# Reading the moving operand of the float32r products from its two halves in turn, in an attention and MLP kernel

## The chip, the cores and the metric

One core of a Trainium2 chip runs the whole kernel. The metric is the device time in microseconds (us) of one execution; the rearranging of inputs and outputs by numpy, ahead of the launch and behind it, is not in it. A time is the median of several executions. For this kernel a difference under 0.3% can't be told from no change.

## The reference

```python
# B, S, D = 4, 3008, 256; z has 64 features; D_FF = 2048
scores = (1.0 / S) * np.matmul(z, z.transpose(0, 2, 1))   # per batch, 3008 x 3008
attn = np.maximum(scores, 0.0) ** 2
x = (u * np.matmul(attn, v)).reshape(B * S, D)
h = x @ w_in
g = h * np.clip(h + 3.0, 0.0, 6.0) / 6.0
y = g @ w_out
```

All of it is float32. The output y has 12032 rows of 256.

## The kernel before

Everything is computed transposed: tokens lie along the free dimension, features along the 128 partitions. TensorE's products are in float32r. To keep float32's precision each operand is split into a rounded high part and the rest (`ah`/`al`, `vh`/`vl`, `xh`/`xl`, `gh`/`gl`, `wi` and `wo` with both parts in one tile), and each product is the sum of three matmuls: low by high, high by low, high by high. All matmuls are made by the helper `mm` (line 75), so in the profile every matmul has line 75 and is known by its tiles.

The tokens of a batch are cut into six chunks of columns: five of 512 and one of 448. For a chunk, the keys are walked in 12 pairs of 128-row blocks. Per pair there are

- the scores (`scores`, `first_scores`): two matmuls `s<-zy,zx` and `s<-zx` for each of the two blocks, into a PSUM bank; then Relu on ScalarE (line 433) from PSUM into the SBUF tile `rt`; then squares on ScalarE and VectorE and the split into `ah`, `al`. The score matrix is symmetric, so many pairs are not computed: the squares of an earlier chunk are kept in DRAM (`keep`), fetched back and transposed on VectorE (`turn`, `from_mirror`). A few pairs are mirrored in one half and computed in the other: the half pairs, whose scores are matmuls of 256 columns (`from_mirror`).
- the product with v (`av`, `first_av`): 12 matmuls `o<-ah,vl`, `o<-ah,vh`, `o<-al,vh` of 512 or 448 columns, that sum over all pairs in the banks `o0`, `o1`. At the end of a chunk, `times_u` multiplies with u (tile `u`).

The MLP runs on pairs of chunks. With the two chunks' columns as halves of 512 or 480 columns, and two halves of the features, `group` does a 2 by 2 block product in seven products instead of eight (`product`, 21 matmuls `m<-xh,wi` and `m<-xl,wi` in all, each with 512 or 480 columns), ScalarE and VectorE put the sums and the gate together in `ra`, `rb`, split them into `gh`, `gl`, and `downs_of` multiplies with `w_out` (matmuls `y<-gh,wo`, `y<-gl,wo`).

The order of the instructions on each engine is written out by hand at the end of the function: the scores run two pairs ahead of the product with v, and from pair 33 on (`MLP_FROM`) one MLP unit is spread over every three pairs; what is left of the MLP runs at the end. Up to that point VectorE also turns the weights, that come as float64, into float32 pieces. Each matmul has its own weight load (PEld in the profile), so there are 8426 of each; ten of these are a warm-up at the start.

The moving operand (`rhs`) of every matmul is read in its natural order: 512 (480, 448, 256) neighbouring float32 words of each partition, one after the other.

Of the kernel before, what the change touches and what calls it, by code (L numbers as in the profile page):

```python
# [10 lines left out]
AF = mybir.ActivationFunctionType  # L11
ALU = mybir.AluOpType

B, S, D, DQK, DFF = 4, 3008, 256, 64, 2048
NT = B * S
P = 128
CH = 512
NCH = 6
# [4 lines left out]
NFP = NF // 2  # L23
# [18 lines left out]
def relu2_attention_then_hswish_mlp(  # L42
# [9 lines left out]
    nc = tc.nc  # L52
# [20 lines left out]

    def mm(out, lhsT, rhs, start, stop, part=False):
        nc.tensor.matmul(out, lhsT=lhsT, rhs=rhs, start=start, stop=stop, skip_group_check=part)  # L75

    def sub(out, a, b):
        nc.vector.tensor_tensor(out=out, in0=a, in1=b, op=ALU.subtract)  # L78
# [337 lines left out]
    def scores(b, c, p, square_on="da", banks="xx"):  # L416


        if is_mirrored(b, c, p):
            yield from from_mirror(b, c, p, banks[1])  # L420
            return
        n = width(c)
        zx, zy = (z[:, :n] for z in zt[b, c])
        rt = rpool.tile([P, 2, CH], F32, tag="r", name="rt")
        rn = rt[:, :, :n]
        for r in range(2):
            s = ps.tile([P, CH], F32, tag=banks[r], name="s")
            j = 2 * p + r
            cols = slice((j % 4) * P, (j % 4) * P + P)
            zj = zt[b, j // 4][0][:, cols]  # L430
            mm(s[:, :n], zj, zy, True, False)
            mm(s[:, :n], zj, zx, False, True)
            nc.scalar.activation(out=rn[:, r], in_=s[:, :n], func=AF.Relu, scale=1.0 / S)  # L433
            if not r:
                yield
        ah = apool.tile([P, 2, CH], F32R, tag="ah", name="ah")
        al = apool.tile([P, 2, CH], F32R, tag="al", name="al")
        hn, ln = ah[:, :, :n], al[:, :, :n]
        keeps = p // 2 > c and (b, p // 2, c) not in DIRECT or is_half(b, c, p + 1) and p // 2 == c
        r2, r_of, r2_of, h_of, l_of = rn, rn, rn, f(hn), ln  # L440
        if keeps or square_on != "aa":
            r2 = r2_of = rpool.tile([P, 2, CH], F32, tag="r", name="r2")[:, :, :n]
        if keeps:
            r_of, r2_of = in_order(rn), by_quadrant(r2)
            h_of, l_of = in_order(f(hn)), in_order(ln)

        def square(on, rows):
            to, of = (r2_of[:, rows], r_of[:, rows])
            if on == "a":
                nc.scalar.activation(out=to, in_=of, func=AF.Square)  # L450
            else:
                nc.vector.tensor_tensor(out=to, in0=of, in1=of, op=ALU.mult)  # L452

        half = 4 if keeps else 1
        if square_on[0] == square_on[1] == "d":
            square("d", slice(None))
        elif square_on[0] == "d":
            square("d", slice(0, half))
        nc.scalar.activation(out=hn, in_=rn, func=AF.Square)  # L459
        if square_on[0] == "a":  # L460
            square("a", slice(None))
        elif square_on[1] == "a":
            square("a", slice(half, None))
        flush_copies()
        if keeps:
            keep(b, c, p, r2)
        yield
        if p < NPAIR - 1:
            sub(l_of, r2_of, h_of)
        else:  # L470
            first, second = (slice(0, 4), slice(4, 8)) if keeps else (0, 1)
            to = in_order(hn) if keeps else hn
            sub(l_of[:, first], r2_of[:, first], h_of[:, first])
            sub(to[64:128, second], r2_of[64:128, second], h_of[64:128, second])
        at[b, c, p] = (ah, al)
        yield

    def first_scores():

        zx, zy = zt[0, 0]  # L480
        rt = rpool.tile([P, 2, CH], F32, tag="r", name="rt")
        r2 = rpool.tile([P, 2, CH], F32, tag="r", name="r2")
        ah = apool.tile([P, 2, CH], F32R, tag="ah", name="ah")
        al = apool.tile([P, 2, CH], F32R, tag="al", name="al")
        at[0, 0, 0] = (ah, al)
        for r in range(2):
            s = ps.tile([P, CH], F32, tag="xy"[r], name="s")
            zj = zx[:, r * P:(r + 1) * P]
            mm(s, zj, zy, True, False)
            mm(s, zj, zx, False, True)  # L490
            nc.scalar.activation(out=rt[:, r], in_=s, func=AF.Relu, scale=1.0 / S)
            nc.scalar.activation(out=ah[:, r], in_=rt[:, r], func=AF.Square)
            nc.vector.tensor_tensor(out=r2[:, r], in0=rt[:, r], in1=rt[:, r], op=ALU.mult)
            sub(al[:, r], r2[:, r], f(ah[:, r]))

    def first_av():

        for d in range(2):
            ot[d] = ps.tile([P, CH], F32, tag=f"o{d}", name=f"o{d}")
        ah, al = at[0, 0, 0]  # L500
        vh, vl = vt[0, 0]
        for k, (a, w, r) in enumerate(
            [(ah, w, r) for r in range(2) for w in (vl, vh)] + [(al, vh, r) for r in range(2)]
        ):
            for d in range(2):
                mm(ot[d], w[:, r, d * P:(d + 1) * P], a[:, r], k == 0, False)

    def width(c):
        return CH if c < NCH - 1 else S - CH * (NCH - 1)
# [1 line left out]
    ot = {}  # L511

    def av(b, c, p, d):

        n = width(c)
        first = p == pairs_of(b, c)[0]
        if first:
            home = f"y0{d}" if (b, c) == (0, 1) else f"o{d}"
            ot[d] = ps.tile([P, CH], F32, tag=home, name=f"o{d}")
        o = ot[d][:, :n]  # L520
        ah, al = at[b, c, p]
        vh, vl = vt[b, p]
        dd = slice(d * P, d * P + P)
        last = p == NPAIR - 1
        passes = [(w, ah, r) for r in range(2) for w in (vl, vh)]
        passes += [(vh, al, r) for r in range(1 if last else 2)]
        for k, (w, a, r) in enumerate(passes):
            mm(o, w[:, r, dd], a[:, r, :n], first and k == 0, last and k == len(passes) - 1)

    raw_x = {}  # L530

# [18 lines left out]
    xt = {}  # L550
# [56 lines left out]
    def downs_of(i, q, gs):  # L607

        n = tokens(i)[1] // 2

        def last_one(h, e):
            o = yt_t[h, e]
            gh, gl = gs[h]
            ee = slice(e * P, e * P + P)
            w = wo[i, q]
            y = rpool.tile([P, 2, CH], F32, tag="r", name="y")[:, e, :n]
            order = (1, 0) if h else (0, 1)
            for r in order:
                mm(o[:, :n], w[:, 1, r, ee], gh[:, r, :n], False, False)
                mm(o[:, :n], w[:, 0, r, ee], gh[:, r, :n], False, False)  # L620
                mm(o[:, :n], w[:, 0, r, ee], gl[:, r, :n], False, r == order[1])
            if e:
                nc.vector.tensor_scalar(
                    out=y, in0=o[:, :n], scalar1=1.0 / 6.0, scalar2=None, op0=ALU.mult
                )
            else:
                nc.scalar.activation(out=y, in_=o[:, :n], func=AF.Copy, scale=1.0 / 6.0)
            t0 = tokens(i)[0] + h * n
            nc.sync.dma_start(out=yt[e * P:(e + 1) * P, t0:t0 + n], in_=y)

        if (i, q) == (NPR - 1, NFP - 1):
            return [(h, e, last_one) for h in range(2) for e in range(2)]

        def one(h, e):
            if q == 0:
                yt_t[h, e] = ps.tile([P, CH], F32, tag=f"y{h}{e}", name=f"y{h}{e}")
            o = yt_t[h, e][:, :n]
            gh, gl = gs[h]
            ee = slice(e * P, e * P + P)
            w = wo[i, q]  # L640
            for r in range(2):
                mm(o, w[:, 1, r, ee], gh[:, r, :n], q == 0 and r == 0, False)
                mm(o, w[:, 0, r, ee], gh[:, r, :n], False, False)
            for r in range(2):
                mm(o, w[:, 0, r, ee], gl[:, r, :n], False, q == NFP - 1 and r == 1)
            if q == NFP - 1 and e == 1:
                store_y(i, h)

        return [(h, e, one) for h in range(2) for e in range(2)]
# [21 lines left out]
    def group(m, x_bank="x", y_bank="y"):  # L671


        i, q = divmod(m, NFP)
        n = tokens(i)[1] // 2
# [3 lines left out]
        w = wi.pop(m)  # L679
# [2 lines left out]
            return ps.tile([P, CH], F32, tag=tag, name="m")[:, :n]  # L682

        def product(o, a, b, start, stop):
            xh, xl = xt[i][b]
            mm(o, w[:, 1, a], xh, start, False, True)
            mm(o, w[:, 0, a], xl, False, False, True)
            mm(o, w[:, 0, a], xh, False, stop, True)
# [24 lines left out]
        y = bank(y_bank)  # L713
# [12 lines left out]
        y = bank(y_bank)  # L726
# [99 lines left out]
    with tc.manual_schedule():  # L826
# [152 lines left out]
        last = (NPR - 1) * NFP - 1  # L979
# [31 lines left out]
_INS = ["zz", "v", "ut", "w_in", "w_out"]  # L1011


# [30 lines left out]
```

## Time and profile before

| | |
|---|---|
| time, median of 3 runs | 1907.8 us (1907.55 to 1912.01) |
| span of the profiled execution, first to last instruction | 1906.0 us, 1.8 us below that median |
| TensorE (PE) busy | 1892.2 us, 99%, 8426 matmuls |
| weight loads (PEld) busy | 1574.6 us, 83% |
| VectorE (DVE) busy | 1510.6 us, 79% |
| ScalarE (ACT) busy | 1199.6 us, 63% |
| granted TensorE clock | 1.000 |

Busy TensorE time is a weak measure here: a matmul's row lasts some 390 ns, but the next begins about 227 ns after it, since they are pipelined. How far apart two matmuls *start* is what counts, and that is read from the timeline.

### The profile page before, as it was taken

To read this page: it belongs to the slowest core of one execution; us is meant where nothing else is said; L and a number is where in the kernel's file an instruction comes from. 1 tells how busy PE (TensorE), PEld (TensorE's weight loads), DVE (VectorE), ACT (ScalarE), POOL (GpSimd) and SP (SyncE) were. 2 spreads that over 40 slices of the span, in tenths; PEclk is the share of its full clock that TensorE was granted. 3 is DMA by queue.
4 is the path that set the end of the run, shared out by engine and by line. 5 is a ranking of instruction groups with operands and counts; after the bars stand their busy time and mean duration, and the time that the engine had idled before them with its cause. 6 is when DMAs were issued, how large, how long until landed. Compare 5 with 4: busy or idle time off the path is not lost.

```text
span 1906.0 us, 23339 instructions
## 1 busy us (share of the span) xinstructions
PE 1892.2 (99%) x8426; PEld 1574.6 (83%) x8426; DVE 1510.6 (79%) x1783; ACT 1199.6 (63%) x1640; POOL 55.5 (3%) x90
## 2 busy tenths in 40 slices
PE   9999999999999999999999999999999999999999
PEld 7877788888888888888888888888888888888887
DVE  8899988878678778887767877888876786787766
ACT  7896656766556556576655655667665565564565
POOL 1000000100000000010000000001000000000000
PEclk9999999999999999999999999999999999999999
DMA  8878978665645675955655666595555567576343
GB/s 232 220 230 219 256 185 219 155 186 184 173 130 163 152 168 120 246 161 174 190 147 138 178 165 162 136 236 156 148 188 137 167 175 171 132 165 161 110 157 121
DMA packets 440307, 329.50 MB, mean 173 GB/s; under 512 B 278656, under 2 KB 397440, under 8 KB 440192
## 3 DMA queue, kind: packets, MB, share of 16 engines
q1 hardware_dynamic: 432672, 304.16, 59.1%
q0 software_dynamic: 7520, 23.86, 4.4%
q8 instruction: 66, 1.08, 0.2%
q14 instruction: 49, 0.40, 0.1%
HBM read 241.70 MB, written 86.25 MB: 172 GB/s over the span
## 4 chain that ended last, share of the span: by engine, by line
PE 66%; issue 23%; DVE 6%; ACT 2%; DMA 2%; SPq 0%; POOL 0%; DVEq 0%; POOLq 0%; ACTq 0%
PE o L75 26%; PE y L75 19%; PE m L75 16%; PE s L75 5%; DVE al L78 1%; DMA l<-d 1%; DVE gl L78 1%; DVE rb L694 0%; DMA dwout<-wh 0%; DVE r L452 0%; DVE rm L373 0%; DMA zraw<-in_zz_dram 0%; DVE xl L78 0%; SPq L334 0%; DVE vl L78 0%
## 5 line engine op out<-in xcount | busy, mean ns | idle before, releaser
L75 PE MATMUL m<-xh,wi 128*128 128x512 f32 (+1 forms) x1344 | 488.6, 387 | 2.8 <-DVE hb L81 1.2
L75 PE MATMUL o<-ah,vl 128*128 128x512 f32 (+1 forms) x1152 | 445.4, 387 | 2.4 <-DVE vl L78 1.2
L75 PE MATMUL o<-ah,vh 128*128 128x512 f32 (+1 forms) x1152 | 444.4, 386 | 0.0
L75 PE MATMUL y<-gh,wo 128*128 128x512 f32 (+1 forms) x1536 | 407.0, 386 | 1.2 <-DMA wo<-dwout 0.7
L75 PE MATMUL o<-al,vh 128*128 128x512 f32 (+1 forms) x1104 | 339.8, 386 | 0.5 <-DVE al L78 0.5
L75 PEld LDWEIGHTS y<-gh,wo 128*128 128x128 f32 x1536 | 288.0, 188 | 57.2 <-ACT gh L754 1.9
L75 PEld LDWEIGHTS m<-xh,wi 128*128 128x128 f32 x1344 | 252.2, 188 | 56.8 <-DVE hb L81 3.6
L75 PE MATMUL m<-xl,wi 128*128 128x512 f32 (+1 forms) x672 | 259.5, 386 | 0.0
L75 PEld LDWEIGHTS o<-ah,vl 128*128 128x128 f32 x1152 | 216.1, 188 | 48.2 <-DVE u L548 3.2
L75 PEld LDWEIGHTS o<-ah,vh 128*128 128x128 f32 x1152 | 216.4, 188 | 42.0
L75 PEld LDWEIGHTS o<-al,vh 128*128 128x128 f32 x1104 | 207.2, 188 | 40.4 <-DVE al L78 0.9
L433 ACT ACTIVATE rt<-s 128x512 f32<-128x512 f32 (+1 forms) x310 | 180.2, 595 | 90.2 <-PE s L75 84.3
L75 PE MATMUL y<-gl,wo 128*128 128x512 f32 (+1 forms) x768 | 234.7, 386 | 0.1
L452 DVE TENSOR_TENSOR r<-rt 128x1024 f32<-128x1024 f32 (+2 forms) x128 | 147.7, 1154 | 99.3 <-ACT rt L433 99.1
L81 DVE TENSOR_TENSOR hb<-hb,m 128x512 f32<-128x512 f32 (+1 forms) x192 | 129.0, 672 | 83.9 <-PE m L75 75.6
L735 ACT ACTIVATE ra<-m,three 128x512 f32<-128x512 f32 (+1 forms) x96 | 65.3, 681 | 198.9 <-PE m L75 195.4
L78 DVE TENSOR_TENSOR al<-r,ah 128x1024 fp32r<-128x1024 f32 (+3 forms) x147 | 164.6, 1120 | 7.1 <-ACT r L450 5.2
L75 PEld LDWEIGHTS y<-gl,wo 128*128 128x128 f32 x768 | 143.9, 188 | 28.5 <-DVE gl L78 0.9
L459 ACT ACTIVATE ah<-rt 128x1024 fp32r<-128x1024 f32 (+1 forms) x155 | 163.8, 1057 | 4.9
L78 DVE TENSOR_TENSOR gl<-rb,gh 128x1024 fp32r<-128x1024 f32 (+2 forms) x97 | 115.4, 1190 | 63.8 <-ACT gh L85 63.2
L78 DVE TENSOR_TENSOR al<-rm,ah 128x1024 fp32r<-128x1024 f32 (+1 forms) x132 | 155.4, 1177 | 1.3 <-ACT ah L400 0.9
L373 DVE STREAM_TRANSPOSE rm<-l 128x1024 f32<-128x1024 f32 (+2 forms) x132 | 149.6, 1133 | 4.1 <-DMA l<-d 4.1
(87 smaller groups left out, 2178.1 us busy)
## 6 DMA issues: line engine op xcount, KB each, us to landing
wi<-dwin SPq DMA_DIRECT2D x96, 896.0 KB, 5.4
d<-r SPq DMA_DIRECT2D x212, 256.0 KB, 3.2
wo<-dwout SPq DMA_DIRECT2D x96, 512.0 KB, 6.1
l<-d SPq DMA_DIRECT2D x304, 128.0 KB, 3.8
l<-d SPq DMA_DIRECT2D x160, 112.0 KB, 4.9
vraw<-in_v_dram POOLq DMA_DIRECT2D x33, 256.0 KB, 3.4
u<-in_ut_dram SPq DMA_DIRECT2D x8, 1024.0 KB, 5.3
out_dram<-y SPq DMA_DIRECT2D x16, 512.0 KB, 5.3
```

What stands on the lines that cost most here:

```text
L75: nc.tensor.matmul(out, lhsT=lhsT, rhs=rhs, start=start, stop=stop, skip_group_check=part)
L78: nc.vector.tensor_tensor(out=out, in0=a, in1=b, op=ALU.subtract)
L81: nc.vector.tensor_tensor(out=out, in0=a, in1=b, op=ALU.add)
L373: nc.vector.transpose(out=rn[:, :, :n].rearrange("p r (k e) -> p r k e", e=32), in_=t[:, :n // 32].rearrange("p k (r e) -> p r k e", r=2),)
L433: nc.scalar.activation(out=rn[:, r], in_=s[:, :n], func=AF.Relu, scale=1.0 / S)
L452: nc.vector.tensor_tensor(out=to, in0=of, in1=of, op=ALU.mult)
L459: nc.scalar.activation(out=hn, in_=rn, func=AF.Square)
L735: nc.scalar.activation(out=ra[:, 1], in_=c21, func=AF.Relu, bias=three)
```

## The change

Two views of a free dimension are added. `paired` reads a tile's columns in the order 0, n/2, 1, n/2+1, and so on: first a column of the left half, then the one at the same place in the right half. All matmuls but the warm-up's and those of the half pairs' scores take their moving operand in that view; what they write to PSUM is still contiguous, but its columns now stand in the paired order. `unpaired` is the reverse view (all even columns, then all odd ones): Relu reads the scores through it, from PSUM, and so writes `rt` in natural order, which the mirrored copies need. The products with v, with `w_in` and with `w_out` leave their columns permuted; the host permutes u to match, and puts the output's rows back in order at the end.

No instruction is added, removed or moved on any engine: the lists of instructions of the two kernels, with line numbers and buffer numbers aside, are the same on all five engines. DMA shapes are the same too.

```diff
+    def paired(ap):
+        return ap.rearrange("p (h n) -> p n h", h=2)
+
+    def unpaired(ap):
+        return ap.rearrange("p (n h) -> p h n", h=2)
+
+    def halved(ap):
+        return ap.rearrange("p (h n) -> p h n", h=2)
...
# scores (first_scores alike)
-            mm(s[:, :n], zj, zy, True, False)
-            mm(s[:, :n], zj, zx, False, True)
-            nc.scalar.activation(out=rn[:, r], in_=s[:, :n], func=AF.Relu, scale=1.0 / S)
+            mm(s[:, :n], zj, paired(zy), True, False)
+            mm(s[:, :n], zj, paired(zx), False, True)
+            nc.scalar.activation(
+                out=halved(rn[:, r]), in_=unpaired(s[:, :n]), func=AF.Relu, scale=1.0 / S
+            )
...
# av (first_av alike)
-            mm(o, w[:, r, dd], a[:, r, :n], first and k == 0, last and k == len(passes) - 1)
+            mm(o, w[:, r, dd], paired(a[:, r, :n]), first and k == 0, last and k == len(passes) - 1)
...
# downs_of (last_one alike)
-                mm(o, w[:, 1, r, ee], gh[:, r, :n], q == 0 and r == 0, False)
-                mm(o, w[:, 0, r, ee], gh[:, r, :n], False, False)
+                mm(o, w[:, 1, r, ee], paired(gh[:, r, :n]), q == 0 and r == 0, False)
+                mm(o, w[:, 0, r, ee], paired(gh[:, r, :n]), False, False)
             for r in range(2):
-                mm(o, w[:, 0, r, ee], gl[:, r, :n], False, q == NFP - 1 and r == 1)
+                mm(o, w[:, 0, r, ee], paired(gl[:, r, :n]), False, q == NFP - 1 and r == 1)
...
# product, in group
-            xh, xl = xt[i][b]
+            xh, xl = (paired(x) for x in xt[i][b])
             mm(o, w[:, 1, a], xh, start, False, True)
             mm(o, w[:, 0, a], xl, False, False, True)
             mm(o, w[:, 0, a], xh, False, stop, True)
...
# host
-        "ut": u.reshape(NT, D).T,
+        "ut": u.reshape(NT, D)[of_u].T,
...
-    return _np.ascontiguousarray(r.results[0]["out_0_dram"].T)
+    y = _np.empty((NT, D), _np.float32)
+    y[of_y] = r.results[0]["out_0_dram"].T
+    return y
```

## Rows read from the trace of the kernel before

**Rows 1.** The page, parts 1 and 2: busy time, and the span in 40 slices.
```profile
PE 1892.2 (99%) x8426; PEld 1574.6 (83%) x8426; DVE 1510.6 (79%) x1783; ACT 1199.6 (63%) x1640; POOL 55.5 (3%) x90
...
DVE  8899988878678778887767877888876786787766
...
PEclk9999999999999999999999999999999999999999
```

**Rows 2.** Timeline of PE, 512 columns each: start us, us, engine line op, tiles, count.
```profile
700.96 0.39 PE L75 MATMUL o<-ah,vl 128*128 128x512 f32 x1
...
702.32 0.39 PE L75 MATMUL m<-xh,wi 128*128 128x512 f32 x1
```

**Rows 3.** Timeline of PE, 512 columns in another stretch, behind matmuls of 480.
```profile
1003.99 0.40 PE L75 MATMUL s<-zy,zx 128*128 128x512 f32 x1
...
1005.85 0.38 PE L75 MATMUL m<-xh,wi 128*128 128x480 f32 x1
```

**Rows 4.** Timeline of PE at the end of the kernel, 480 columns.
```profile
1896.67 0.59 PE L75 MATMUL y<-gh,wo 128*128 128x480 f32 x2
...
1901.21 0.59 PE L75 MATMUL y<-gh,wo 128*128 128x480 f32 x2
```

**Rows 5.** Timeline of PE, 448 columns.
```profile
322.46 0.36 PE L75 MATMUL o<-ah,vl 128*128 128x448 f32 x1
...
323.68 1.09 PE L75 MATMUL y<-gh,wo 128*128 128x512 f32 x4
```

**Rows 6.** Timeline of PE, a half pair's scores, 256 columns.
```profile
284.59 0.28 PE L75 MATMUL s<-zy,zx 128*128 128x256 f32 x1
284.70 0.28 PE L75 MATMUL s<-zx 128*128 128x256 f32 x1
...
285.06 0.40 PE L75 MATMUL o<-ah,vl 128*128 128x512 f32 x1
```

**Rows 7.** Groups by line and shape, PE: count, busy us, mean ns, idle before; first and last.
```profile
L75 PE MATMUL o<-ah,vl 128*128 128x512 f32 x960 | 375.0, 391 | 1.8 <-DVE vl L78 1.2 <-DVE u L548 0.6
...
L75 PE MATMUL s<-zy,zx 128*128 128x448 f32 x16 | 5.8, 364 | 0.0
```

**Rows 8.** Who waited for whom: engine, tile, releaser, us in total, times, longest.
```profile
DVE r L452 <- ACT rt L433: 99.1, 71, 3.0
...
PE warm L75 <- DVE three L829: 1.5, 1, 1.5
...
PE m L75 <- DVE hb L81: 1.2, 2, 1.0
...
PE s L75 <- DVE zx L78: 0.3, 1, 0.3
```

**Rows 9.** Busy time of PE, PEld, DVE, ACT, POOL (count) by stretches of the span.
```profile
0.00:100.00 100.00, 96.86 (x409) 77.47 (x410) 86.86 (x133) 83.57 (x123) 10.67 (x21) 1.00 0.85 229
100.00:200.00 100.00, 97.23 (x419) 77.29 (x418) 97.33 (x150) 77.19 (x108) 5.71 (x8) 1.00 0.79 227
200.00:250.00 50.00, 47.96 (x208) 38.44 (x207) 44.46 (x68) 31.20 (x43) 2.14 (x3) 1.00 0.88 234
...
400.00:1900.00 1500.00, 1498.78 (x6715) 1254.11 (x6714) 1152.92 (x1286) 909.24 (x1232) 24.88 (x39) 1.00 0.60 162
```

**Rows 10.** The same, of line 433 (Relu) alone: ScalarE busy us (count).
```profile
0.00:100.00 100.00, 27.86 (x48) 1.00 0.85 229
100.00:200.00 100.00, 14.57 (x26) 1.00 0.79 227
```

**Rows 11.** Groups by line and shape, ScalarE and VectorE: busy us, mean ns, idle before.
```profile
L433 ACT ACTIVATE rt<-s 128x512 f32<-128x512 f32 x294 | 171.9, 598 | 88.4 <-PE s L75 82.9 <-DVE al L78 4.1 <-DMA wo<-dwout 0.8
L459 ACT ACTIVATE ah<-rt 128x1024 fp32r<-128x1024 f32 x147 | 156.2, 1063 | 4.7
...
L140 DVE TENSOR_SCALAR wraw<-wraw 128x512 uint32<-128x512 uint32 x16 | 6.8, 423 | 0.3
...
L131 DVE TENSOR_SCALAR t<-wraw 128x512 uint32<-128x512 uint32 x16 | 6.7, 417 | 0.1
```

More of the change, by code (lines that the diff above doesn't have):

```diff
@@ L488, in first_scores @@
             zj = zx[:, r * P:(r + 1) * P]
-            mm(s, zj, zy, True, False)
-            mm(s, zj, zx, False, True)
-            nc.scalar.activation(out=rt[:, r], in_=s, func=AF.Relu, scale=1.0 / S)
+            mm(s, zj, paired(zy), True, False)
+            mm(s, zj, paired(zx), False, True)
+            nc.scalar.activation(
+                out=halved(rt[:, r]), in_=unpaired(s), func=AF.Relu, scale=1.0 / S
+            )
             nc.scalar.activation(out=ah[:, r], in_=rt[:, r], func=AF.Square)
@@ L505, in first_av @@
             for d in range(2):
-                mm(ot[d], w[:, r, d * P:(d + 1) * P], a[:, r], k == 0, False)
+                mm(ot[d], w[:, r, d * P:(d + 1) * P], paired(a[:, r]), k == 0, False)
     def width(c):
@@ L618, in last_one @@
             for r in order:
-                mm(o[:, :n], w[:, 1, r, ee], gh[:, r, :n], False, False)
-                mm(o[:, :n], w[:, 0, r, ee], gh[:, r, :n], False, False)
-                mm(o[:, :n], w[:, 0, r, ee], gl[:, r, :n], False, r == order[1])
+                mm(o[:, :n], w[:, 1, r, ee], paired(gh[:, r, :n]), False, False)
+                mm(o[:, :n], w[:, 0, r, ee], paired(gh[:, r, :n]), False, False)
+                mm(o[:, :n], w[:, 0, r, ee], paired(gl[:, r, :n]), False, r == order[1])
             if e:
@@ L1011, with _paired, _orders @@
 _INS = ["zz", "v", "ut", "w_in", "w_out"]
+def _paired(a):
+    return a.reshape(2, -1).T.reshape(-1)
+def _orders():
+    import numpy as _np
+    widths = [CH] * (NCH - 1) + [S - CH * (NCH - 1)]
+    of_u = _np.concatenate([
+        b * S + c * CH + _paired(_np.arange(w)) for b in range(B) for c, w in enumerate(widths)
+    ])
+    of_y = _np.concatenate([
+        _paired(_paired(half))
+        for b in range(B)
+        for c in range(0, NCH, 2)
+        for half in of_u[b * S + c * CH:b * S + c * CH + widths[c] + widths[c + 1]].reshape(2, -1)
+    ])
+    return of_u, of_y
 def kernel(**inputs):
@@ L1021 @@
     u, v, z = (_np.asarray(inputs[k]) for k in "uvz")
+    of_u, of_y = _orders()
     zt = z.transpose(0, 2, 1)
```

## The prediction

> **What bounds the kernel now.** First the page: TensorE is busy 99% of the span and its granted clock is full in every slice; VectorE has 79%, ScalarE 63% [rows 1]. So what counts is how closely the matmuls follow one another, and what makes TensorE wait.
>
> The list of waits answers the second: the longest entry of TensorE, apart from the warm-up, is 1.2 us in two waits [rows 8]. All twelve entries of PE together are 9.6 us. Of the 13.8 us in which TensorE isn't busy at all [rows 1], 8 lie in the first 250 us [rows 9]. There is little to win in waits.
>
> The first is read from the timeline, from start to start. Six matmuls of 512 columns follow from 700.96 to 702.32, so 1.36 / 6 = 226.7 ns each [rows 2]. The granted clock is 1.00 [rows 1], which is the upper of its two levels, 2.4 GHz, and one column per cycle would be 512 / 2.4 = 213.3 ns. So 13.3 ns per matmul are lost while nothing waits. The same at other widths:
> - 480 columns: 21 matmuls from 1896.67 to 1901.21, 216.2 ns against 200.0: 16.2 lost [rows 4].
> - 448 columns: six in 1.22 us, 203.3 against 186.7: 16.7 lost [rows 5].
> - 256 columns: four in 0.47 us, 117.5 against 106.7: 10.8 lost; but the first of them takes only 0.11 us, about 3 ns over its columns [rows 6].
>
> What is this loss? It hardly grows with the columns, so it looks like a price per matmul. But it isn't a constant of the instruction: behind some 480-column matmuls, eight of 512 columns take from 1003.99 to 1005.85, 232.5 ns each [rows 3], against 226.7 elsewhere [rows 2], with the same tiles and no wait. A price that changes with how the matmuls lie in time is what two streams give that get in each other's way. There are two that always run together: the moving operand of a matmul, and the next matmul's weights, 1574.6 us of weight loads in all, one to each matmul [rows 1]. Both come out of SBUF. I take the loss to be such collisions, and the moving operand's reads one side of them. This is inferred from the spread alone.
>
> **What the change does, and its cost.** It moves no instruction and adds none; it changes in which order a matmul's columns are fetched, and how Relu reads.
>
> *The fetches.* With the paired order, neighbouring columns come from two places a half tile apart instead of one place. No row shows a moving operand read so; the bounds are these. From below: a matmul can't be faster than its columns, so at best all 13.3, 16.2 and 16.7 ns are saved. In the middle: nothing changes. From above: each fetch of two neighbours becomes two fetches, and the stream runs at half the rate; that is a rival, below. I take the side of a gain, because the matmuls' loss changes with how the two streams lie (rows 2 against rows 3), and the paired order changes just that. What remains I take as 3 ns per matmul, from the smallest step that any row shows, the half pair's first [rows 6].
>
> The counts come from the groups by shape, twenty groups of which the first and the last are shown [rows 7]: 6312 matmuls of 512 columns, 1440 of 480, 600 of 448; another 64 of 256 columns aren't changed, nor are the ten of the warm-up. The sum:
> - 6312 x (226.7 - 216.3) = 65.6 us
> - 1440 x (216.2 - 203.0) = 19.0 us
> - 600 x (203.3 - 189.7) = 8.2 us
>
> Together 92.8 us. The stretches at 232.5 would add to that; I leave them out, since I don't know their share.
>
> *Given back.* A faster TensorE sooner waits for the others. From 100 to 200 us VectorE is busy 97.3 of 100 us, and TensorE's 419 matmuls there would gain 419 x 10.4 ns = 4.4 us, while VectorE has 2.7 left [rows 9]; I take 2 us of that as lost. From 0 to 100 and 200 to 250 us VectorE is at 87% and 89%, and each wait there gets somewhat longer: 1 us. From 400 to 1900 us it has 347 us of 1500 free, and ScalarE 591, so a stretch that is 5% shorter has room: 2 us for new waits over all of it. Together 5 us.
>
> *Relu.* It reads each second word of a PSUM bank. 512 more elements cost ScalarE 1063 - 598 = 465 ns [rows 11], so if skipping cost as much as reading, each Relu would take 465 ns more; from below, nothing. The nearest row is on another engine and memory: VectorE reading and writing each second word of a weight tile, 423 ns against 417 for the step beside it, which only reads them so [rows 11]. Neither is slower than the other, so a step of two words in the output costs nothing; I take nothing for Relu. At the upper end it would matter in the first 200 us alone: 74 Relus there [rows 10], 34 us more on a ScalarE that has 39 us left of 200 [rows 9], and VectorE already waits 99.1 us in all for Relu [rows 8]; I put this end at up to 15 us. Later ScalarE is busy 61% [rows 9], the scores are made two pairs ahead, and it stays hidden.
>
> *The sum.* 92.8 - 5 = 88 us. The profiled span is 1906.0 us, so 1818 us, and with the 1.8 us by which the median stands above it, **1820 us**.
>
> *A rule beside it.* The Trainium skill, TensorE: Matmul & The Clock Gate, section "Wait — 56ns, not 53.3ns?", gives 215.7 ns from start to start for back-to-back matmuls of 512 columns at the upper clock, 2.5 ns over the columns. Rows 2 don't agree for this kernel (226.7). By that figure in place of my 3 ns, the sum would be about 4 us lower, an estimate from that page.
>
> **The rivals.**
>
> *The stream runs at half the rate (slower).* The place is every paired matmul. If two neighbouring words are fetched together today, and the paired order needs a fetch for each, 512 columns take 427 ns, 480 take 400 and 448 take 373. That is 6312 x 200 + 1440 x 184 + 600 x 170 = 1629 us more: about **3535 us**. It decides from a small price on: more than the 13 to 17 ns that are lost now, 0.05 to 0.07 ns for each pair of columns, makes the kernel slower. For it: no row of the trace shows an operand of TensorE whose neighbouring columns lie apart, so nothing excludes it. Against it: VectorE's rows with a step of two words show no loss [rows 11], though that is a short step. The Trainium skill, Advanced Engine Details and Errata, section "SBUF Cachelines", speaks for this rival: lines are 16 bytes long, at least two hits on a line are needed to absorb the memory's latency, and a different line at each access costs. Four neighbouring columns share a line now, and with the paired order no two in a row do. No run here shows that rule for TensorE; by the 423 and 417 ns, two hits per line are free, which agrees as far as it goes.
>
> *The reads aren't the cause (no change).* The loss is the price of exchanging the weights, one load per matmul, and the order of the columns leaves it as it is. For it: it is nearly the same for 448, 480 and 512 columns. Against it: 226.7 and 232.5 ns for the same width. Time: **1908 us**, and up to 1923 us if Relu is at its upper end, too.
>
> *Only a part is won.* The streams still collide, but half as often: 46 us off, less 3 given back, **1865 us**.
>
> **How the numbers follow.** I give the forecast 0.62, the partial gain 0.10, no change 0.08, Relu's cost without a gain 0.02, and the half rate 0.18. The half rate gets so much because no row excludes it; the gain gets most because the loss is there in each matmul, isn't fixed, and waits for nothing else. Faster by over 0.3% (below 1902 us) is 0.72, within 0.3% 0.08, slower 0.20.
>
> The forecast's own range is 1794 to 1848 us. Its low end takes the whole 118 us (6312 x 13.3 + 1440 x 16.2 + 600 x 16.7, so 84 + 23 + 10), less 4 given back; its high end takes 6 ns per matmul in place of 3, which is 25 us more, and a few more waits. To leave no more than 2 in 10 out, the range reaches over the partial gain and no change, to 1912 us. The half rate lies outside.
>
> **What would show it.** The timeline: a matmul of 512 columns starts some 216 ns after the one before it, of 480 some 203, and the 232.5 ns stretches are gone; the half pairs stay at 117.5. If the steps are unchanged, the loss isn't in the reads; at 427 the pairs were fetched together. Line 433's successor shows Relu's price: 598 ns or up to 1063. In the list of waits TensorE's total rises by about 5 us, mostly for VectorE's `hb`, `al` and `vl` before 250 us. Wrong would make the forecast: a new wait of TensorE for Relu, over 10 us in all; or steps that are shorter while the span isn't, which would put the bound on VectorE.

## The result, and the profile after

The changed kernel takes 1840.8 us (median of 4, 1838.5 to 1842.3) against 1907.9 of before: a ratio of 0.9645, 95% interval 0.9631 to 0.9658. That is 67 us less, where 88 were forecast. The profiled execution is the slowest of the four (1842.3 us).

The page of the changed kernel, parts 1 and 2 (beside [rows 1]):

```profile
span 1840.5 us, 23339 instructions
...
PE 1801.9 (98%) x8426; PEld 1584.1 (86%) x8426; DVE 1518.5 (83%) x1783; ACT 1197.3 (65%) x1640; POOL 55.8 (3%) x90
...
DVE  8999998888778778897867877889887787887776
...
PEclk9999999999999999999999999999999999999999
```

TensorE is still busy nearly all the time, but 38.6 us of the span are idle now (1840.5 - 1801.9), where 13.8 were. VectorE's busy time has grown by 7.9 us, though it does the same work.

Timeline of PE after the change, first 512 columns (beside [rows 2]), then 480 (beside [rows 4]):

```profile
690.01 0.38 PE L75 MATMUL o<-ah,vl 128*128 128x512 f32 x1
...
693.89 0.38 PE L75 MATMUL o<-ah,vl 128*128 128x512 f32 x1
...
1782.19 0.97 PE L75 MATMUL y<-gh,wo 128*128 128x480 f32 x4
...
1785.84 0.37 PE L75 MATMUL m<-xh,wi 128*128 128x480 f32 x1
```

Eighteen matmuls start from the first row of either pair up to the second: 3.88 / 18 = 215.6 ns at 512 columns, 3.65 / 18 = 202.8 at 480. A step is the time from one matmul's start to the next one's. Over all steps of the trace that hold no wait, the means are 215.8, 202.6 and 189.2 ns (512, 480, 448 columns), where the kernel before has 227.7, 216.6 and 202.5. So each paired matmul stands 2.5 ns over its columns, whatever its width and whatever is around it; the stretches of 232 ns [rows 3] are gone. By these means the steps alone are worth 6312 x 11.9 + 1440 x 14.0 + 600 x 13.3 = 103 us. The span fell by 65.5, so 38 us were given back.

Where, is seen from the busy time by stretches (beside [rows 9]); the last two rows are two short stretches:

```profile
0.00:100.00 100.00, 94.02 (x413) 77.99 (x414) 90.97 (x133) 84.84 (x126) 10.76 (x21) 1.00 0.86 233
100.00:200.00 100.00, 88.96 (x393) 72.63 (x393) 98.42 (x142) 73.55 (x102) 5.94 (x8) 1.00 0.71 213
200.00:250.00 50.00, 46.26 (x212) 39.25 (x211) 48.94 (x74) 29.87 (x43) 1.29 (x2) 1.00 0.87 235
...
345.00:349.00 4.00, 3.87 (x12) 3.19 (x11) 4.00 (x6) 2.51 (x4) 0.00 (x0) 0.59 0.86 338
1659.50:1663.50 4.00, 4.00 (x13) 3.41 (x13) 3.72 (x5) 1.47 (x3) 0.00 (x0) 0.57 0.94 286
```

In the first 250 us TensorE makes 413 + 393 + 212 = 1018 matmuls; before it made 1036 [rows 9]. Nothing is won there, though each step is shorter: VectorE is busy 98.4 of the second 100 us, and 48.9 of the next 50. Matmul number 900 starts 3.4 us later than before, and number 1500, at 359 us, still 4.2 us later; only from there on does the changed kernel draw ahead, by 65 us at the end. The two short stretches show something that the kernel before doesn't have: the granted clock is 0.59 and 0.57 on the mean, which is the lower of its two levels, 1.2 GHz, for most of them. The steps in the two are 3.4 us longer in all than at the upper level. Just ahead of each lies a long step of TensorE (1.8 us at 342 us, 2.4 us at 1657), where the longest before the change is 1.4 us. Such a step alone doesn't bring it about: after two others of 2.4 us, at 245 and 310 us, the clock stayed at the upper level.

Who makes TensorE wait (beside [rows 8]):

```profile
PE o L75 <- DVE u L564: 7.8, 6, 2.1
PE m L75 <- DVE hb L93: 6.1, 6, 2.0
PE o L75 <- DVE al L90: 4.3, 6, 1.5
PE o L75 <- DVE vl L90: 2.7, 4, 1.0
...
DVE rm L385 <- DMA l<-d: 8.5, 4, 2.6
```

All entries of PE are 33.5 us together, where they were 9.6. 26.5 us of them are waits for VectorE (some 7 before), 6.6 for ScalarE (2 before). The last row is VectorE's own wait for a mirrored pair out of DRAM, which before the change was:

```profile
DVE rm L373 <- DMA l<-d: 4.1, 4, 1.5
```

It comes back below.

Relu through the strided view costs nothing (beside [rows 11]; 598 ns before):

```profile
L445 ACT ACTIVATE rt<-s 128x512 f32<-128x512 f32 x294 | 171.8, 596 | 71.2 <-PE s L75 65.0 <-DVE al L90 4.3 <-DMA wo<-dwout 0.6
```

But some of VectorE's groups have become slower. Groups by shape of VectorE before, and then after:

```profile
L78 DVE TENSOR_TENSOR al<-r,ah 128x1024 fp32r<-128x1024 f32 x117 | 142.7, 1220 | 6.2 <-ACT r L450 5.0
...
L152 DVE SCALAR_TENSOR_TENSOR wraw<-wraw 128x512 f32<-128x512 uint32 x16 | 11.0, 688 | 0.3
L136 DVE SCALAR_TENSOR_TENSOR t<-wraw,t 128x512 uint32<-128x512 uint32 x16 | 11.0, 687 | 0.3
```

```profile
L90 DVE TENSOR_TENSOR al<-r,ah 128x1024 fp32r<-128x1024 f32 x117 | 142.5, 1218 | 2.8 <-ACT r L464 1.6
...
L164 DVE SCALAR_TENSOR_TENSOR wraw<-wraw 128x512 f32<-128x512 uint32 x16 | 14.2, 889 | 0.3
L148 DVE SCALAR_TENSOR_TENSOR t<-wraw,t 128x512 uint32<-128x512 uint32 x16 | 13.4, 835 | 0.3
...
L152 DVE TENSOR_SCALAR wraw<-wraw 128x512 uint32<-128x512 uint32 x16 | 8.7, 544 | 0.3
```

`al` takes what it took, as VectorE's other large contiguous groups do. The seven conversion steps of a weight tile, that read or write each second word of `wraw`, take 78.1 us in all instead of 64.2, and they stand in the part where VectorE binds: they run until 247 us. The MLP begins at 133 us, so they don't end where it begins, as the section on the kernel before has it.

### The profile page after: what moved, and what is told of

Same layout as the page of the kernel before. It is cut to its first block, busy times and chain, and to the rows that moved or that the text cites. A ratio compares the mean times of both kernels' runs of the same rounds, so it can differ in the third digit from the quotient of the medians.

```text
span 1840.5 us, 23339 instructions
## 1 busy us (share of the span) xinstructions
PE 1801.9 (98%) x8426; PEld 1584.1 (86%) x8426; DVE 1518.5 (83%) x1783; ACT 1197.3 (65%) x1640; POOL 55.8 (3%) x90
## 4 chain that ended last, share of the span: by engine, by line
issue 46%; PE 37%; DVE 11%; ACT 3%; DMA 3%; SPq 1%; POOL 1%; DVEq 0%; POOLq 0%; ACTq 0%
PE o L75 14%; PE y L75 10%; PE m L75 9%; PE s L75 3%; DVE al L90 2%; DMA zraw<-in_zz_dram 1%; DVE gl L90 1%; DMA l<-d 1%; DVE rb L710 1%; DVE rm L385 1%; ACT gh L770 1%; DVE ra L710 1%; DVE r L466 1%; DVE hb L93 1%; SPq L346 0%
## 5 line engine op out<-in xcount | busy, mean ns | idle before, releaser
L75 PE MATMUL m<-xh,wi 128*128 128x512 f32 (+1 forms) x1344 | 476.9, 378 | 11.1 <-DVE hb L93 6.1
L75 PE MATMUL o<-ah,vl 128*128 128x512 f32 (+1 forms) x1152 | 433.1, 376 | 10.6 <-DVE u L564 7.8
L75 PE MATMUL o<-ah,vh 128*128 128x512 f32 (+1 forms) x1152 | 431.9, 375 | 0.0
L75 PE MATMUL y<-gh,wo 128*128 128x512 f32 (+1 forms) x1536 | 388.6, 375 | 1.9 <-ACT gh L770 1.8
L75 PE MATMUL o<-al,vh 128*128 128x512 f32 (+1 forms) x1104 | 328.8, 376 | 4.3 <-DVE al L90 4.3
L75 PE MATMUL m<-xl,wi 128*128 128x512 f32 (+1 forms) x672 | 252.5, 376 | 0.0
L75 PE MATMUL y<-gl,wo 128*128 128x512 f32 (+1 forms) x768 | 226.7, 376 | 1.0 <-DVE gl L90 0.5
```

## The experiments

Times are medians; each has runs of the kernel before beside it on its chip (1907.6 to 1909.0 us), and the ratios are to those.

**The order of reading, by itself.** A kernel of matmuls alone, forty to a chain, each with its own weight load, one chain per order (`x` is the moving tile, `w` the weights, `m` the columns of weights, `k` is 40):

```python
        def paired(t, n=CH):
            return t[:, :n].rearrange("p (h n) -> p n h", h=2)
...
        def near(k):
            return lambda t: t[:, :CH].rearrange("p (m h n) -> p m n h", h=2, n=k)
...
            for i in range(k):
                ww = w[:, (i % 4) * P:(i % 4) * P + m]
...
                nc.tensor.matmul(
                    o[:m, :n], lhsT=ww, rhs=rhs(x), start=i == 0, stop=i == k - 1,
                    skip_group_check=True,
                )
...
        run("nat", natural)
        run("pair", paired)
...
        run("w32", natural, m=32)
...
        run("near4", near(4))
```

A second kernel of the same form has further orders. Each of the two was run once.

> TensorE alone: chains of 40 matmuls (256 or 512 columns, a new weight load each), one chain per order of reading; nothing of the reference is computed, and only two tiles of output are written. All at the upper clock after 60 matmuls. Theory (the moving operand's reads and the next weights' reads get in each other's way): natural order 226 to 232 ns from start to start, halves in turn 215.8; with weights of 64 and 32 columns in natural order the loss of about 13 ns shrinks to about half and a quarter, so some 221 and 218 ns. Rival (the moving operand's reads alone lose, the weights have no part): 64 and 32 columns of weights stay at 226 to 232 ns. Rival (another engine's traffic causes it in the kernel): natural order takes 216 ns here, where no other engine works. Line rule (neighbouring reads in different lines cost): a step of four words takes 427 ns or more, a step of two about as much as natural; two or four neighbours of one half and then of the other would not be slower than one and one. Without the rule all steps are alike.

> TensorE alone again, chains of 40 matmuls in further orders; nothing of the reference is computed. What the first chains showed (natural 226.7 ns, with 32 columns of weights still 231.7, in turn from two places at any distance from 4 words on 215.8) leaves the moving operand's own reads as the place of the loss. Theory (neighbouring words of one place, read one after the other, stall; words in turn from two places don't, whatever the weights): with 32 columns of weights, 256 columns natural take 114 to 120 ns and in turn 109; 480 in turn 202.5; 480 and 448 natural 212 to 221 and 199 to 207. Starting one or two words later changes nothing for either order. Two words apart (in turn within one line of 16 bytes) is slow, since both reads fall on one line. In turn with a step of four words inside each half, so that each read needs a new line, is slower than 216 ns; with a step of two it is the question. bfloat16 natural, half the bytes for each column, takes 215.8. Rival (what counts is only that the pattern's innermost run has two words): in turn at a distance of two words, and with steps inside the halves, also 215.8. Line rule (each change of line costs): the steps of the in-turn orders are ranked by the lines that they touch.

Timeline of PE in the first of these kernels; a name's number is left out, so `w` is the chains with 64 and 32 columns of weights, `near` those in turn at a distance of 4 and of 16 words, `step` those with a step of 2 and of 4 words:

```profile
24.57 9.23 PE L46 MATMUL nat<-x,w 128*128 128x512 f32 x40
33.64 8.80 PE L46 MATMUL pair<-x,w 128*128 128x512 f32 x40
42.27 9.25 PE L46 MATMUL nat_b<-x,w 128*128 128x512 f32 x40
...
84.42 18.62 PE L46 MATMUL w<-x,w 128*64 128x512 f32 x80
102.88 8.80 PE L46 MATMUL w_pair<-x,w 128*64 128x512 f32 x40
111.51 11.48 PE L46 MATMUL four<-x,w 128*128 128x512 f32 x40
122.83 17.43 PE L46 MATMUL near<-x,w 128*128 128x512 f32 x80
140.10 36.67 PE L46 MATMUL step<-x,w 128*128 128x512 f32 x80
176.58 9.58 PE L46 MATMUL wstep<-x,w 128*128 128x512 f32 x40
```

From one row's start to the next: natural (33.64 - 24.57) / 40 = 226.8 ns, in turn (42.27 - 33.64) / 40 = 215.8. The same of the second kernel, with 32 columns of weights (`n256w`, `n128w`) and in bfloat16 (`bf`; one of its records is missing):

```profile
124.90 4.89 PE L49 MATMUL n256w<-x,w 128*32 128x256 f32 x40
129.63 4.53 PE L49 MATMUL n256w_pair<-x,w 128*32 128x256 f32 x40
133.99 2.56 PE L49 MATMUL n128w<-x,w 128*32 128x128 f32 x40
136.40 2.40 PE L49 MATMUL n128w_pair<-x,w 128*32 128x128 f32 x40
138.63 16.99 PE L49 MATMUL n<-x,w 128*128 128x480 f32 x80
...
163.56 8.81 PE L49 MATMUL bf<-xb,wb 128*128 128x512 bf16 x39
172.21 19.54 PE L49 MATMUL bf_pair<-xb,wb 128*128 128x512 bf16 x40
191.58 8.79 PE L49 MATMUL bf_near<-xb,wb 128*128 128x512 bf16 x40
200.03 9.47 PE L49 MATMUL end<-x,w 128*128 128x512 f32 x40
```

Chain by chain, the mean from start to start within it, without its first few steps, from the same traces (512 columns and 128 columns of weights where nothing else is said):

| order, float32r | ns |
|---|---|
| natural; the same with 64 and with 32 columns of weights | 226.7; 230.2; 231.7 |
| natural, weights read with a step of four words | 235.1 |
| natural, begun one word, two words later | 236.6; 233.3 |
| two halves in turn; with 64 columns of weights; begun a word later | 215.8; 215.9; 216.6 |
| in turn from places 4, 8, 16 words apart | 215.8; 215.8; 215.9 |
| in turn from places 2 words apart | 227.6 |
| 2, 4, 32 words of one half, then of the other | 340.0; 250.1; 236.5 |
| four, eight places in turn | 283.3; 486.7 |
| one place, with a step of 2, of 4 words | 451.1; 461.3 |
| two halves in turn, with a step of 2, of 4 words in each | 227.4; 453.4 |
| 480 columns: natural, in turn; 448 columns: natural | 216.7, 202.5; 202.7 |
| 256 columns: natural, in turn; with 32 columns of weights | 120.0, 111.7; 117.8, 109.2 |
| 128 columns, 32 columns of weights: natural, in turn | 60.0; 55.8 |

In bfloat16 the natural order takes 215.8 ns, the two halves in turn 484.4, and in turn at 4 words (8 bytes) 215.8.

What follows. The loss is there with no other engine at work, so it isn't their traffic. It doesn't shrink with the weights: with a quarter of their columns it is 231.7 - 213.3 = 18 ns rather than 13. So the theory of collisions with the weight loads falls in the form in which the expectation has it, which put that chain at 218 ns. With few weights the loss goes with the columns: in turn saves 4.2 ns at 128, 8.6 at 256 and 15.9 at 512 (there against the chain in turn with all weights), some 8% each time. So it goes with the moving operand's own reads, and their order ends it. The weights are not without a part: fewer of them (230.2 and 231.7) or weights read with a step (235.1) make the natural order slower. How large their part is stays open, since no chain without new weights was run. Where the operand begins matters too: one or two words later, the natural order takes 236.6 and 233.3 ns, where the second expectation had no change. Taking words in turn from two places that are four words or more apart ends it, at any distance tried; two words apart doesn't. The rival that only a run of two words counts falls by that 227.6, and by 453.4 with a step of four. More than two places, or short runs from each, cost far more than they save. The line rule of the first expectation misses: a step of two words, which it had about as fast as natural, takes 451.1 ns, and short runs from each half are slower than one word and one. Why the reads behave so is not settled by this table. In bfloat16 the natural order has no such loss, and two halves in turn more than double the time.

**One part alone.** The MLP's matmuls paired and attention's not, with Relu as before, and the reverse (with the host's permutations to match):

```diff
# e_mlp_only
-            mm(s[:, :n], zj, paired(zy), True, False)
+            mm(s[:, :n], zj, zy, True, False)
...
-            mm(o, w[:, r, dd], paired(a[:, r, :n]), first and k == 0, last and k == len(passes) - 1)
+            mm(o, w[:, r, dd], a[:, r, :n], first and k == 0, last and k == len(passes) - 1)
# e_att_only
-            xh, xl = (paired(x) for x in xt[i][b])
+            xh, xl = xt[i][b]
...
-                mm(o, w[:, 0, r, ee], paired(gh[:, r, :n]), False, False)
+                mm(o, w[:, 0, r, ee], gh[:, r, :n], False, False)
```

> Only the MLP's matmuls (4320 of 8416) read in turn from halves; attention and Relu as before. By the steps of the changed kernel's trace (215.8 instead of about 227.5 ns at 512 columns, 202.5 instead of 216.5 at 480) this is worth 34 + 20 = 54 us before any give-back. Theory (what is given back is given back to VectorE in the first 250 us, where there is little MLP): most of it stays, 1862 to 1870 us. Rival (each matmul's gain is given back in the same proportion everywhere, 67 of 102): about 1872.

> Only attention's matmuls (4032) and Relu are changed; the MLP as before. Worth by steps 41 + 8 = 49 us before give-back. Theory (VectorE binds in the first 250 us, where most matmuls are attention's): about 13 us of it can't be won there, and some later; 1872 to 1882 us. Rival (proportional give-back): about 1876; if Relu's strided read cost something, above 1885.

Measured: MLP alone 1872.9 us, 0.9815 (0.9798 to 0.9831); attention alone 1880.7 us, 0.9861 (0.9845 to 0.9877). The two parts save 1.85% and 1.39%, together 3.24% of the 3.55% of both: each part brings a share of its own. Of what their steps are worth (54 and 49 us by the expectations) 35 and 27 us were measured, 35% and 45% less. The MLP's number is the proportional rival's, so the theory that nearly all is given back in the first 250 us falls in that form; attention's is in its theory's range and 5 us above that rival. But not all of the difference was given back in waits: in each kernel the matmuls left in natural order became slower. With the MLP paired, attention's steps of 512 columns take 229.7 ns on the mean, where they took 227.8, and those of 448 columns 203.9 instead of 202.5, which is 7 us of the 19 that are missing; with attention paired, the MLP's take 228.8 instead of 227.5 at 512 columns and 217.2 instead of 216.6 at 480, 4.5 us of 22. So neither number measures the waits alone. Line 164, the slowed conversion step, in these two kernels:

```profile
L164 DVE SCALAR_TENSOR_TENSOR wraw<-wraw 128x512 f32<-128x512 uint32 x16 | 11.9, 745 | 0.3
```

```profile
L164 DVE SCALAR_TENSOR_TENSOR wraw<-wraw 128x512 f32<-128x512 uint32 x16 | 13.0, 814 | 0.3
```

745 ns with the MLP paired and 814 with attention paired, between 688 with nothing and 889 with all. When it slows shows what slows it. Up to 137 us, about where the MLP begins, its nine executions take 686 to 696 ns with the MLP paired, and 834 to 960 ns with attention paired. Behind that, with the MLP paired, six of the other seven take 743 to 935 ns. The step slows while paired matmuls run, and not before.

**VectorE's load taken away.** Six of the seven conversion steps of each weight tile left out, in the changed kernel and in the one before:

```diff
         nc.vector.tensor_scalar(
-            out=t0, in0=top, scalar1=0x07FFFFFF, scalar2=3,
-            op0=ALU.bitwise_and, op1=ALU.logical_shift_left,
+            out=t0, in0=top, scalar1=0x01FFFFFF, scalar2=None, op0=ALU.bitwise_and
         )
-        yield
-        nc.vector.scalar_tensor_tensor(
...
+        for _ in range(7):
+            yield
```

> The changed kernel with six of the seven VectorE steps that turn each weight tile from float64 to float32 left out (96 instructions, some 56 us of VectorE, all in the first 430 us); the weights are then wrong. Theory (the gain that is missing is lost to VectorE in the first part): 15 to 30 us under the changed kernel, 1811 to 1826. Rival (it is lost to DMA, ScalarE or the clock): within 6 us of 1841.

> The same steps left out of the kernel before. Theory: TensorE's matmuls bind it, and its waits before 250 us are some 13 us, so it gains at most about 10 us: 1896 to 1904; the distance between the two kernels grows from 67 to 80 us or more. Rival: the distance stays at 67.

Measured: the changed kernel falls to 1824.2 us (0.9554, 0.9538 to 0.9570), the one before to 1904.1 (0.9977, 0.9968 to 0.9987). Both are where the theory had them: 17 us for the one, 4 for the other, and the distance grows from 67 to 80 us. What was left out isn't the same in both: 70 us of VectorE in the changed kernel, 57 in the one before. Stretches of the changed kernel without these steps:

```profile
0.00:100.00 100.00, 96.67 (x429) 82.11 (x430) 73.48 (x107) 87.09 (x130) 11.40 (x22) 1.00 0.91 243
100.00:200.00 100.00, 96.05 (x428) 80.81 (x426) 75.34 (x105) 76.75 (x107) 4.98 (x7) 0.98 0.82 229
```

VectorE is busy 73 and 75 of 100 us there instead of 91 and 98, and TensorE makes 429 and 428 matmuls instead of 413 and 393. Behind the first 1000 matmuls nothing comes back: what TensorE loses there by waits is 29.8 us in this kernel's trace and 30.2 in the changed kernel's. So 23 of the 103 us that the steps are worth stay missing without this load.

**Attempts to win it back.** The subtractions of the weights' low parts on GpSimd; the MLP three pairs earlier; one conversion step on ScalarE; the conversion spread later; the mirrored pairs fetched earlier; and the changed kernel again beside the last two.

```diff
# v_pool
-            sub(l, of, f(h))
+            nc.gpsimd.tensor_tensor(out=l, in0=of, in1=f(h), op=ALU.subtract)
# v_early
-MLP_FROM = 33
+MLP_FROM = 30
...
-                if SPLIT_FROM <= g < SPLIT_FROM + 9:
-                    run(xs, 1)
-                if g == SPLIT_FROM + 8:
+                if SPLIT_FROM <= g < SPLIT_FROM + 5:
+                    run(xs, 2)
+                if g == SPLIT_FROM + 5:
# v_abs
-        nc.vector.tensor_scalar(
-            out=top, in0=top, scalar1=0x7FFFFFFF, scalar2=None, op0=ALU.bitwise_and
-        )
+        nc.scalar.activation(out=f1, in_=f1, func=AF.Abs)
# v_rate, in build_rate
-        return 0 if g < 2 else 2 if g < 4 else 1 if g < 12 else 3 if g < 18 else 4 if g < MLP_FROM else 5
+        return 0 if g < 2 else 2 if g < 4 else 1 if g < 12 else 3 if g < 14 else 2 if g < 30 else 5
# v_fetch, in background
                     turn_next()
+                    if i or p > 9:
+                        fetch_mirrored()
```

> The changed kernel, with the subtractions that make the weights' low parts (32 instructions, some 18 us of VectorE, all before 430 us) on GpSimd. Theory (VectorE's load in the first part takes the gain): up to 6 us faster than the changed kernel, 1833 to 1841. Rival (GpSimd gets in VectorE's way or is late with the weights): 1841 or slower.

> The changed kernel, with the MLP's units begun three pairs earlier (30 instead of 33, its first inputs split in five pairs instead of nine), so that there is more TensorE work in the part in which VectorE binds. Theory: 1 to 6 us faster than the changed kernel, 1835 to 1840. Rival (VectorE has even more to do in these pairs): 1841 to 1848.

> The changed kernel, with one of the seven conversion steps of each weight tile (16 instructions, 6.8 us of VectorE) on ScalarE as an absolute value. Theory: 1 to 4 us faster than the changed kernel, 1837 to 1840. Rival (the chain of steps now crosses engines and waits): 1841 or slower.

> The changed kernel, with the weights' conversion spread later: two steps in place of four in each pair from 14 to 29, five from 30 on. Theory (VectorE binds from 100 to 250 us and has 14% left from 250 to 400): 3 to 8 us faster than the changed kernel, 1833 to 1838. Rival (the load comes back where the MLP has begun): 1840 or slower.

> The changed kernel, with the fetch of the next mirrored pair issued right behind the transposition that frees its buffer, half a pair earlier than now. Theory (a part of what is given back behind 250 us comes from VectorE waiting for such a fetch, 8.5 us in four waits, with TensorE queued behind it at the start of the last chunk of a batch): 3 to 8 us faster than the changed kernel, 1833 to 1838. Rival (these waits are only where VectorE's load shows, or the earlier fetch holds up the weights' fetches on the same queue): 1840 or slower.

> The changed kernel once more, beside the two others on the same chip: 1838 to 1843 us.

| kernel | us | ratio to before, 95% interval |
|---|---|---|
| changed kernel again | 1844.3 | 0.9662 (0.9649 to 0.9675) |
| v_fetch | 1840.1 | 0.9638 (0.9624 to 0.9652) |
| v_rate | 1856.6 | 0.9728 (0.9715 to 0.9741) |
| v_abs | 1844.0 | 0.9656 (0.9642 to 0.9669) |
| v_pool | 1845.8 | 0.9666 (0.9653 to 0.9679) |
| v_early | 1852.3 | 0.9699 (0.9685 to 0.9712) |

The changed kernel again came out at 1844.3 us, 1.3 us above the range that was expected of it, and 3.5 above its first result (the intervals of their ratios overlap). v_pool, v_early and v_abs ran on another chip than the other three, so the ratios are compared. v_abs and v_pool are no different from the changed kernel, and v_early and v_rate are slower; in all four the theory's numbers failed. Moving VectorE's work about didn't help in these four ways:

- On GpSimd the 512-wide subtractions take 1985 and 1444 ns instead of 705 and 690, and beside them VectorE's seven conversion steps take 86.8 us in all instead of 78.5.
- With one step on ScalarE, TensorE waits less for VectorE in the profiled run (19.0 us instead of 26.9 in the changed kernel again), but more for ScalarE (19.8 instead of 6.4). That run is the slowest of its six, 1853.0 us.
- With the MLP begun earlier, or the conversion spread later, the two meet. Both kernels have a wait of TensorE that the changed kernel doesn't have, 6.3 us (v_early) and 5.9 (v_rate), where its longest is 2.1. In v_rate ScalarE stands 5.3 us there, waiting for VectorE's subtractions for the weights, and TensorE waits for the Relu behind that. VectorE's busy share from 250 to 400 us is no higher there than in the changed kernel (126 and 129 of 150 us), so this looks like the order of the work rather than a lack of free time, which no run separates. From 200 to 400 us, TensorE makes 189 + 615 matmuls instead of 212 + 681.

v_fetch is 4 us faster than the changed kernel on the same chip, but at 1840.1 us it lies in its rival's numbers, the intervals overlap, and 0.2% is less than this measurement tells apart. So whether it gains is not shown. Its trace has what was meant; VectorE's wait for a mirrored pair (8.5 us in four waits in the changed kernel):

```profile
DVE rm L385 <- DMA l<-d: 1.1, 1, 1.1
```

How such a wait reaches TensorE is seen in the changed kernel's timeline:

```profile
1208.06 1.11 DVE L385 STREAM_TRANSPOSE rm<-l 128x896 f32<-128x896 f32 x1 [1.89 <-DMA l<-d]
...
1209.09 1.18 DVE L710 SCALAR_TENSOR_TENSOR rb<-rb,hb 128x1024 f32<-128x1024 f32 x1
...
1210.19 0.68 DVE L564 TENSOR_TENSOR u<-u,o 128x512 f32<-128x512 f32 x1
...
1210.93 0.46 PE L75 MATMUL o<-ah,vl 128*128 128x448 f32 x1 [1.38 <-DVE u L564]
```

The transposition waits for the fetch, the gate and the product with u stand behind it on VectorE, and TensorE waits for the bank that this product frees. VectorE's four waits end at 310, 760, 1208 and 1656 us, and each has a long step of TensorE with it (2.4, 1.3, 1.8 and 2.4 us, 7 us more in all than steps without a wait). The kernel before has four such waits of VectorE too, 4.1 us in all, and none of TensorE's steps there is over 1 us. In v_fetch's profiled run the granted clock's mean is 1.000, and no stretch at the lower level is left; but that holds for two of its five runs alone, its fastest (1834.6 and 1836.4 us), while the other three have 0.998. Of the changed kernel's eight runs, six have 0.997 or 0.998.

## Why the prediction came out as it did

- *The side, and where it comes from:* right. Every step of the sum was taken from start-to-start times, and these fell as forecast: 216.3 was put down for 512 columns, 215.8 came; 203.0 for 480, 202.6 came; 189.7 for 448, 189.2 came. The remainder of 3 ns, read off one row of a half pair, was 2.5. That is the figure that the page TensorE: Matmul & The Clock Gate of the Trainium skill gives (section "Wait — 56ns, not 53.3ns?"); the trace after the change agrees with it, where the one before didn't.
- *The gain of the steps:* mis-sized a little, 92.8 us forecast, 103 by the means over all steps. Slower stretches such as that at 232.5 ns, which the sum left out because their share wasn't known, make some 6 of these 10 us, and the remainder of 2.5 in place of 3 ns the other 4.
- *What the loss is:* wrong in its reason. The collisions with the next matmul's weights fell in the form forecast: the loss stays with a quarter of the weights. "It hardly grows with the columns, so it looks like a price per matmul" was a misreading of four rows; with little weight load it is 8% of the columns' time at 128, 256 and 512. The half pairs, on which that reading leaned, still take 118.7 ns in the changed kernel; a chain of the same width with all weights loaded takes 111.7 even in turn, where 109.2 are to be had with few, so at 256 columns the weight loads have a share. What held was the narrower inference, that the loss sits in the moving operand's reads and moves with their order. That this very order ends it was partly luck: nothing in the reasoning says that two places in turn are free where four cost 283 ns, and bfloat16 loses by it.
- *Given back:* this is the term that failed, 5 us forecast and 38 measured. Summing by how much steps with a wait are longer than the others, the first 1000 matmuls lost 12.8 us before and 27.4 after, the others 7.6 and 30.2. So 15 us were given back in the first 240 us, where 3 were put down, and 23 later, where 2 were. Two thoughts behind the 5 us were too kind. First, VectorE's 2.7 free microseconds of 100 were counted as usable, and its durations as fixed; but its seven conversion steps became 13.9 us longer. That VectorE's load holds TensorE up there is shown by leaving six of the steps out: 17 us in the changed kernel, 4 in the one before. How much of the 15 us comes from the longer durations, and how much from TensorE's asking sooner, is not shown. The prediction's own sign of being wrong, shorter steps with the bound on VectorE, is what these first 350 us show. Second, "347 us free of 1500" is a mean over stages. Behind 400 us TensorE's steps of over 1.1 us come at the same places of each batch, 448 us apart: at 587, 1035 and 1483 us for `hb`, which stands behind other work on VectorE, and at 762, 1209 and 1657 behind VectorE's wait for a mirrored pair. Of the 23 us, 7 are in the four long steps behind such waits (the first at 310 us), and 3.4 in the two stretches at the lower clock. The rest is spread over many short waits, and no run takes it apart.
- *The number:* the two errors pull opposite ways. Steps worth 10 us more than forecast made up for a part of the 33 us by which the given-back term was short; that 1840.8 us lies in the forecast's own range of 1794 to 1848 us owes something to this. (The low end's 118 us are 84 + 23 + 10 = 117.)
- *Relu at nothing:* right, 596 ns against 598. The row it was taken from, VectorE's step of two words in SBUF, says nothing of ScalarE's reading from PSUM, so this came right without support.
- *The half rate:* its price was about right, but not for this order. 451 to 487 ns is what a step of two or four words, eight places in turn, or bfloat16 halves in turn take. By the Trainium skill's line rule (Advanced Engine Details and Errata, "SBUF Cachelines") the paired order should cost, since no two neighbouring reads share a line, and a step of two words should not; the chains show 215.8 and 451.1, the reverse. With a step of four, a new line for each word, they agree with it (461.3).
- *No change, or half the gain:* neither. The loss went down to 2.5 ns, and the time that is missing went to waits and to the stretches at the lower clock.

What stays open is why two places in turn are free and one place isn't, and why VectorE's strided steps slow down beside paired matmuls. Neither an experiment that changes only these steps' stride nor a chain that loads no new weights was made.

## What to carry to other kernels

Where TensorE is busy all the time, compare the time from start to start with columns over clock: the difference can be a reading order that costs 5% in float32r and shows in no list of waits. Try such an order in a chain of matmuls first, in the kernel's own type: the order that frees float32r more than doubles the time in bfloat16. And when a bound engine becomes faster, look for the stage where another one has no room, rather than at its mean: here over a third of what the matmuls gained was given back, about half of it in waits for VectorE.

## What the runs showed of the hardware

- A float32r matmul of 512 neighbouring words takes 226.7 to 236.6 ns from start to start, and 215.8 when the words come in turn from two places at least four words apart; more places cost more (283.3 for four, 486.7 for eight). In bfloat16 the natural order takes 215.8 and two halves in turn 484.4.
- A moving operand with a step of two words takes twice the time (451.1 ns), nearly as much as one with a step of four (461.3).
- ScalarE reads each second word of a PSUM bank as fast as neighbouring ones (596 and 598 ns).
- VectorE's steps on each second word of an SBUF tile became 17 to 29% slower beside paired matmuls (from 690 to 807 ns the least, from 688 to 889 the most, on the mean), and only while such matmuls ran; contiguous ones of 1024 columns stayed at 1218 to 1220 ns.
- Twice in the profiled run of the changed kernel the granted clock stood at the lower level (0.59 and 0.57 on the mean of 4 us), shortly after a step of TensorE of 1.8 and of 2.4 us, and matmuls of 512 columns then took 427 ns; after two other steps of 2.4 us it stayed at the upper one.
